# One fused attention, feed-forward and expert kernel: a longer first chunk of the feed-forward, other routing groups, and zero products between the first attention steps

## The chip, the core and the metric

The kernel runs on one core of one Trainium2 chip, in one launch. The metric is the time of that launch on the device in microseconds (us). Five instruction streams run beside each other and wait for each other on semaphores: TensorE (PE in the profile, its weight loads PEld), VectorE (DVE), ScalarE (ACT), GpSimd (POOL) and SyncE (SP, which issues most DMAs). Each stream is executed in its written order.

## The reference

Three stages follow each other; everything is float32. N is 1536 tokens of 512 numbers.

```python
# 1 attention, 2 x 8 heads x 768 x 64: 8 global keys and a local window of 96, linear bias
scores = scale * q @ k.T + bias;  scores = where(keep, scores, -1e9)
a = exp(scores - max);  a = a / (sum(a) + 1e-9);  x = a @ v        # -> 1536 x 512
# 2 gated feed-forward, d_ff = 1536
xn = x / sqrt(mean(x * x) + 1e-6) * rms_g
x = (silu(xn @ w_gate) * (xn @ w_val)) @ w_out
# 3 the two best of 8 experts, 512 -> 1024 -> 512
noisy = x @ w_gate2 + log1p(exp(x @ w_noise)) * noise
top2 = the two largest of noisy;  weight = softmax over the two
out[token] += weight * (relu(x @ w1[e]) @ w2[e])                   # for both experts e
```

## The kernel before

Tokens are handled in 12 tiles of 128 rows. A product of high accuracy is made of three products of two halves each (high x high, high x low, low x high), so most of what TensorE does comes in threes.

**Order of the work.** The program is written with pools of tiles; a scheduler with a timeline of its own estimates (a list scheduler) then decides the order of the instructions on each engine. What the source fixes is what is to be computed, what depends on what, which buffer pool a tile takes, and in which order the pieces get their priority. The order that it made is known before anything runs and can be printed; the times that it had in mind are not used here.

**Attention** is cut into 48 units (tile, pair of heads), which `slot` emits in four steps that lag behind each other: `prep` (L313, transposes of K and Q), `scores` (L363 products `ps`, then VectorE adds the bias and takes the row maximum, L367, then ScalarE's exponential), `turn` (L383, transposes `pp` of the probabilities, copied out by ScalarE and VectorE) and `values` (L428 or L432, products `po`). The first START = 12 units run with nothing else on TensorE ("wide"; they may use more PSUM banks). After that, units are laid between the products of the feed-forward.

**Feed-forward.** d_ff is 12 blocks of 128. The blocks are grouped in CHUNKS; a visit is (chunk, first tile, number of tiles), and VISITS lists them. For each block of a visit `up` makes the gate and value products (L592), `hidden` the gated value on ScalarE and VectorE (`u`, then `dh` and `dl`, its two halves), and `down` the products with w_out (L619), which collect in PSUM over the blocks of the chunk and are then added to the tile's sum `x2` (L629). Chunk 0 takes two tiles per visit (256 columns per product) and runs beside the attention; the later chunks mostly take four tiles (512 columns). The weights come as 64-bit words; `conv` takes them apart on ScalarE, VectorE and GpSimd, and FEED says how many pieces each visit converts. Converted weights lie in pool "a" and, once attention is finished and its memory free, in pool "b" (NRAW says how many).

**Routing.** The tiles are routed in groups GS. `route(g)` follows the last `down` of its tiles: transposes of x2 (L669), router logits `lg` (L673), two ScalarE functions with table loads, the two best of eight on VectorE (`ny` to `chosen`, `sel`), products with a triangle of ones that count how many tokens each expert has before this one (L700 to L703), the slot number `si`, and one indirect DMA per tile and choice from GpSimd that scatters token number and weight to a table in DRAM (L749, `metad`). After group LEAD = 1 (tiles 0 to 7) the kernel counts which expert leads (L715, `lead`), SP loads that number, and unit 0 is prepared: SP fetches the leader's first 256 table entries (`me`, L788, which waits for the scatters), VectorE makes the indices `ic` (L797), GpSimd gathers the rows of x2 (L806), TensorE transposes them (L816).

**Experts.** Unit 0 is the leader's first 256 slots and unit 1 the rest of it; the other experts follow. Unit 1's list must hold tokens of the very last group, which `late_slots` patches in (L644 to L658: `idf` reads the fetched `me`, four comparisons `hot`, 16 small products). Weights of a unit come by SP into raw slots `wab` (L772, L775) and are split into halves (`sa`, `sb`, L576 and L578).

All DMAs of SP stand in one stream: the stores of x2 to DRAM (L632), the fetches of `me` and the weights. A waiting one holds up all that follow.

Of the kernel before, what the change touches and what calls it, by code (L numbers as in the profile page):

```python
# [19 lines left out]
P = 128  # L20
# [85 lines left out]
def fused(ctx: ExitStack, tc: tile.TileContext, q, k, v, n_global, n_local, w_gate, w_val, w_out,  # L106
# [12 lines left out]
    FB2 = F2 // P  # L119
    GS = [4, 4, 2, 2]  # L120
    NG = len(GS)
    G0 = [sum(GS[:g]) for g in range(NG)]
    LEAD = 1
    ST = 4
    CHUNKS = [[0, 1, 2], [3, 4, 5], [6, 7], [8, 9, 10, 11]]
    VISITS = [(0, 2 * i, 2) for i in range(6)] + [(1, 4 * i, 4) for i in range(3)]
    VISITS += [(c, t, 4) for c in (2, 3) for t in (0, 4)] + [(2, 8, 4), (3, 8, 2), (3, 10, 2)]
    FEED = [0, 0, 1, 0, 2, 2, 2, 2, 2, 3, 3]
    START = 12
    LAG = 8  # L130
    NRAW = {"a": 12, "b": 8}
    NACC = 8
# [71 lines left out]
    def small_loads():  # L204
        nc.scalar.dma_start(grow, rms_g.rearrange("(o d) -> o d", o=1).broadcast_to([P, DM]))
        nc.scalar.dma_start(wr[:, :, :E], w_router.rearrange("(c p) e -> p c e", p=P))
        nc.scalar.dma_start(wr[:, :, E:], w_noise.rearrange("(c p) e -> p c e", p=P))
        nc.scalar.dma_start(nz, noise.rearrange("(t p) e -> p t e", p=P))
    tri = sb.tile([P, P], BF16, name="tri")
    ones = sb.tile([P, P], BF16, name="ones")  # L210
# [54 lines left out]
    def bank(kind, wide, name):  # L265
        tags = {"s": ("g", "s"), "t": ("t", "t2", "v"), "o": ("o", "d")} if wide else {"s": ("s",), "t": ("t", "t2"), "o": ("o",)}
        cyc[kind] += 1
        tag = tags[kind][cyc[kind] % len(tags[kind])]
        return ps.tile([P, 512], F32, name=name, tag=tag, bufs=2 if tag == "d" else 1)
# [77 lines left out]
    def scores(u, wide):  # L347
# [9 lines left out]
        for t in range(2):  # L357
            h = pair[pr][t]
            sl = slice((h % 2) * D, (h % 2 + 1) * D)
            o = psc[:, t * W:(t + 1) * W]  # L360
            prods = ((0, 0), (1, 0), (0, 1)) if ti >= F32T else ((0, 0),)
            for n, (a, c) in enumerate(prods):
                nc.tensor.matmul(o, qT[a][sl, h // 2, :], kT[c][sl, h // 2, C0:], start=(n == 0), stop=(n == len(prods) - 1))  # L363
        for t in range(2):
# [10 lines left out]
    def turn(u, wide):  # L375
# [5 lines left out]
        for t in range(2):  # L381
            for j in range(nblk):
                nc.tensor.transpose(p4[:, t, j, :], pp[t][:, j * P:(j + 1) * P], ident)  # L383
        if ti < F32T:
# [143 lines left out]
    def conv(nm, f, src):  # L528
# [11 lines left out]
        sh = nc.vector.tensor_scalar(wi, wi, 3, 0x3FFFFFF8, op0=ALU.logical_shift_left, op1=ALU.bitwise_and)  # L540
        if late:
            after(ab, "A", 1)
            after(sh, "V", 1)
        nc.vector.scalar_tensor_tensor(wi, hi, -0x40000000, wi, op0=ALU.bitwise_and, op1=ALU.bitwise_or)
# [50 lines left out]
    def hidden(ci, f, t0, nt, pg, pv):  # L595
        GN = nt * P
        hp = pools.get("b", at)
        wd = 512 if "b" in pools else 256
        u = hp.tile([P, wd], F32, name=f"u{t0}_{f}", tag="u", bufs=1)[:, :GN]
        nc.scalar.activation(u, pg, AF.Tanh, scale=0.5)  # L600
        nc.vector.scalar_tensor_tensor(u, u, 1.0, pg, op0=ALU.add, op1=ALU.mult)
        nc.vector.scalar_tensor_tensor(u, u, 0.5, pv, op0=ALU.mult, op1=ALU.mult)  # L602
        dh = hp.tile([P, wd], F32R, name=f"dh{t0}_{f}", tag="dh", bufs=2)
        dl = hp.tile([P, wd], F32R, name=f"dl{t0}_{f}", tag="dl", bufs=2)
        nc.scalar.activation(dh[:, :GN], u, AF.Copy)  # L605
        (nc.gpsimd if ci < len(CHUNKS) - 1 else nc.vector).tensor_sub(dl[:, :GN], u, dh[:, :GN].bitcast(F32))  # L606
        return dh, dl

    def down(ci, t0, nt, f, d):
# [12 lines left out]
        for t in range(nt):  # L622
# [7 lines left out]
            if ci == len(CHUNKS) - 1:  # L630
                x2t[ti] = accs[ti]
                nc.sync.dma_start(x2d[ti * P:(ti + 1) * P, :], accs[ti])  # L632
        if t0 + nt == NT // P:
# [26 lines left out]
    def route(g):  # L660
# [3 lines left out]
        for t in range(GT):  # L664
            ti = G0[g] + t
            pt = ps.tile([P, 512], F32, name=f"pr{ti}", tag="ts"[t % 2 if last else 0])
            p3 = pt.rearrange("p (a b) -> p a b", a=DC)
# [241 lines left out]
    while n < START:  # L909
        slot(n, 0)  # L910
        slot(n, 1)
        if n in (3, 6, 9):
            feed(3)
        n += 1
    prev = None
    todo = []
# [13 lines left out]
    def finish(ci, t0, nt, f, d):  # L930
        down(ci, t0, nt, f, d)
        if ci == len(CHUNKS) - 1 and f == CHUNKS[ci][-1] and t0 != G0[-1]:
            g = G0.index(t0)
            route(g)
            if g == LEAD:
                r = nc.sync.value_load(lead.bitcast(I32)[:1, :1], min_val=0, max_val=E - 1)
                units[0].e = units[1].e = r
            if g == LEAD + 1:
                units[1].fetch()

    for vi, (ci, t0, nt) in enumerate(VISITS):
# [9 lines left out]
        for f in CHUNKS[ci]:  # L951
# [19 lines left out]
            prev = (ci, t0, nt, f, d)  # L971
            if (ci, t0) == (2, 8):
                if f == CHUNKS[ci][1]:
                    units[0].slots()
                    units[0].gather(0)
                    units[0].gather(1)
            if ci == 3 and t0 >= 8:
                k = CHUNKS[ci].index(f) + (4 if t0 == 10 else 0)
                if k in (2, 3):
                    units[0].turn(k - 2)  # L980
                moe2_weights(0, units[0].e, k)
    finish(*prev)
# [116 lines left out]
```

## Time and profile before

| what | value |
|---|---|
| median of 3 runs | 856.24 us (855.93 to 857.28) |
| profiled execution | 857.62 us |
| its span, first to last instruction | 855.8 us |
| TensorE busy | 802.3 us (94%) |
| VectorE, ScalarE, GpSimd busy | 54%, 41%, 36% |
| mean granted TensorE clock | 0.960 |

A granted clock of 1.00 in a row is TensorE's full level, 0.50 the lower one; a value between is a mean over both. TensorE's busy time counts an instruction's whole stay in the pipeline, so that a busy engine may still make half its products when the clock is low. The clock of a window is 1.00, too, in the first 36 us, where the trace holds no record of it; there the durations tell it. A row's idle time in square brackets stands just before the instruction, with what ended it.

### The profile page before, as it was taken

The page shows a single profiled execution, that of the slowest core. Times are in us where ns is not written, and L with a number is a line of the kernel's source. Part 1 is how long each engine was busy: PE and PEld are TensorE (multiplying, and loading weights), DVE is VectorE, ACT ScalarE, POOL GpSimd, SP SyncE. Part 2 cuts the span into 40 slices and gives each one's busy share as a digit, 9 for nine tenths or more (in the row PEclk, how much of TensorE's full clock was granted, in tenths as well). Part 3 has the DMA queues.
Part 4 walks back from the last instruction along what each step waited for, and adds up shares of the span by engine and source line. Part 5 has one row for each costly group of instructions (what it writes and reads, how often), then busy time and mean ns, then how long its engine had stood idle before and what let it go on. Part 6 is the DMA issues. An engine that isn't in the chain of part 4 may idle for free. (4 is left out here: it accounts for less than half of the span.)

```text
span 855.8 us, 13326 instructions
## 1 busy us (share of the span) xinstructions
PE 802.3 (94%) x4824; PEld 700.5 (82%) x4824; DVE 462.7 (54%) x1032; ACT 350.6 (41%) x780; POOL 304.7 (36%) x340
## 2 busy tenths in 40 slices
PE   5999999999899999999999777999999999999993
PEld 4678889888778888888889566888899999999982
DVE  3867855675688766323345344654445454545551
ACT  4656665565453332111313252553334343343440
POOL 5335532231665553000053233341242433435321
PEclk9969998999899999999999895999999999999997
DMA  9424431170132420001010505477072829082710
GB/s 200 138 75 136 123 76 26 39 198 2 53 120 99 146 62 15 1 1 50 1 51 21 155 23 124 161 217 221 25 245 77 246 81 278 36 272 91 237 44 33
DMA packets 117125, 89.79 MB, mean 105 GB/s; under 512 B 49481, under 2 KB 100681, under 8 KB 117056
## 3 DMA queue, kind: packets, MB, share of 16 engines
q1 hardware_dynamic: 106864, 68.24, 28.4%
q0 software_dynamic: 7440, 20.32, 7.0%
q10 hardware_dynamic: 2752, 0.34, 0.3%
q8 instruction: 40, 0.66, 0.3%
q14 instruction: 29, 0.24, 0.1%
HBM read 76.23 MB, written 13.34 MB: 105 GB/s over the span
## 5 line engine op out<-in xcount | busy, mean ns | idle before, releaser
L842 PE MATMUL pz<-gh,sa 128*128 128x256 f32 (+7 forms) x576 | 160.1, 344 | 10.1 <-issue 8.6
L842 PEld LDWEIGHTS pz<-gh,sa 128*128 128x128 f32 x576 | 105.6, 192 | 17.0 <-issue 8.6
L842 PE MATMUL pz<-gl,sa 128*128 128x256 f32 (+7 forms) x288 | 98.4, 342 | 0.0
L619 PE MATMUL acc<-wo,dh 128*128 128x512 f32 x288 | 89.3, 403 | 2.8 <-ACT dh L605 2.8
L858 PE MATMUL ac<-zh,sb 128*128 128x480 f32 (+4 forms) x320 | 85.8, 361 | 0.0
L606 POOL TENSOR_TENSOR dl<-u,dh 128x256 fp32r<-128x256 f32 (+1 forms) x33 | 35.4, 1074 | 130.9 <-ACT dh L605 122.2
L846 ACT ACTIVATE zh<-pz 128x256 fp32r<-128x256 f32 (+7 forms) x72 | 35.1, 487 | 108.6 <-PE pz L842 94.8
L847 DVE SCALAR_TENSOR_TENSOR zl<-pz,zh 128x256 fp32r<-128x256 f32 (+7 forms) x72 | 39.7, 552 | 68.4 <-ACT zh L846 55.4
L576 ACT ACTIVATE sa<-wab 128x512 fp32r<-128x512 f32 x72 | 45.3, 629 | 76.2 <-PE ac L858 19.4
L578 POOL TENSOR_TENSOR sa<-wab,sa 128x512 fp32r<-128x512 f32 x21 | 27.1, 1290 | 119.0 <-ACT sa L576 118.1
L619 PEld LDWEIGHTS acc<-wo,dh 128*128 128x128 f32 x288 | 53.0, 191 | 14.1 <-ACT dh L605 3.0
L578 DVE TENSOR_TENSOR sa<-wab,sa 128x512 fp32r<-128x512 f32 x51 | 36.5, 716 | 49.1 <-ACT sa L576 38.5
L592 PE MATMUL pg<-xTh,wg 128*128 128x512 f32 x184 | 62.0, 398 | 0.2 <-DVE u L602 0.2
L592 PE MATMUL pv<-xTh,wv 128*128 128x512 f32 x184 | 61.7, 396 | 0.0
L858 PEld LDWEIGHTS ac<-zh,sb 128*128 128x128 f32 x320 | 59.0, 188 | 3.0
L842 PEld LDWEIGHTS pz<-gl,sa 128*128 128x128 f32 x288 | 55.2, 192 | 2.7
L363 PE MATMUL ps<-kT,qT 64*128 64x256 f32 (+1 forms) x248 | 54.2, 368 | 2.1 <-DVE mx L367 1.4
L619 PE MATMUL acc<-wo,dl 128*128 128x512 f32 x144 | 54.6, 405 | 0.0
L370 ACT ACTIVATE p<-s,mx 128x256 f32<-128x256 f32 (+1 forms) x96 | 46.2, 483 | 19.6 <-DVE mx L367 19.3
L864 PE MATMUL ac<-sb,zh 128*128 128x512 f32 (+1 forms) x160 | 51.4, 407 | 1.4 <-ACT sb L576 1.4
L858 PE MATMUL ac<-zl,sb 128*128 128x480 f32 (+4 forms) x160 | 52.7, 358 | 0.0
L578 DVE TENSOR_TENSOR sb<-wab,sb 128x512 fp32r<-128x512 f32 x67 | 46.7, 697 | 7.6 <-ACT sb L576 7.0
(227 smaller groups left out, 1855.9 us busy)
## 6 DMA issues: line engine op xcount, KB each, us to landing
wab<-in_moe_w_dram SPq DMA_DIRECT2D x128, 256.0 KB
rg<-in_moe_w_gate_dram SPq DMA_DIRECT2D x12, 512.0 KB
rv<-in_moe_w_val_dram SPq DMA_DIRECT2D x12, 512.0 KB
ro<-in_moe_w_out_dram SPq DMA_DIRECT2D x12, 512.0 KB
kn<-in_k_dram SPq DMA_DIRECT2D x12, 256.0 KB
qn<-in_q_dram SPq DMA_DIRECT2D x12, 256.0 KB
vn<-in_v_dram SPq DMA_DIRECT2D x12, 256.0 KB
out_dram<-zero SPq DMA_DIRECT2D x1, 3072.0 KB
```

What stands on the lines that cost most here:

```text
L363: nc.tensor.matmul(o, qT[a][sl, h // 2, :], kT[c][sl, h // 2, C0:], start=(n == 0), stop=(n == len(prods) - 1))
L370: nc.scalar.activation(p[:, :W], s[:, :W], AF.Exp, scale=-1.0, bias=mx[:, h:h + 1], accum_out=sm[:, h:h + 1])
L576: nc.scalar.activation(wp[:, 0], src, AF.Copy)
L578: (nc.gpsimd if pool else nc.vector).tensor_sub(wp[:, 1], src, wp[:, 0].bitcast(F32))
L592: nc.tensor.matmul(pz, a[:, cs], x[:, tt:tt + nt, c, :], start=(n == 0), stop=(n == 3 * DC - 1))
L606: (nc.gpsimd if ci < len(CHUNKS) - 1 else nc.vector).tensor_sub(dl[:, :GN], u, dh[:, :GN].bitcast(F32))
L619: nc.tensor.matmul(acc[t], a[:, tt], w, start=(f == CHUNKS[ci][0] and n == 0), stop=(end and n == 2))
L842: nc.tensor.matmul(pz[:, :cap], a[:, cs], x[:, c, :cap], start=(k == 0), stop=(k == 3 * DC - 1))
L846: nc.scalar.activation(dh[:, :cap], pz[:, :cap], AF.Relu)
L847: nc.vector.scalar_tensor_tensor(dl[:, :cap], pz[:, :cap], 0.0, dh[:, :cap].bitcast(F32), op0=ALU.max, op1=ALU.subtract)
L858: nc.tensor.matmul(acc[c][:, :cap], w[:, c * P:(c + 1) * P], a[:, :cap], start=(f == 0 and k == 0), stop=(f == FB2 - 1 and k == 2))
L864: nc.tensor.matmul(acc[s][:m], a[:, ss], w, start=(f == 0 and k == 0), stop=(f == FB2 - 1 and k == 2))
```

## The change

- Chunks and visits: chunk 0 gets four blocks instead of three, chunk 1 two (blocks 4 and 5). The visits (3, 4) and (2, 8) of four tiles become two visits of two tiles each. FEED and NRAW follow.
- Two-tile visits take their `u`, `dh` and `dl` always from the pool `sb`, no longer from the pool that opens when attention has ended.
- `conv` of block 1 is ordered behind the normalisation of tile 0, that of block 2 behind tile 1, that of later blocks behind tile 2 (before: from block 2 on behind tile 1).
- Routing groups of 4, 2, 2, 2 and 2 tiles instead of 4, 4, 2 and 2; LEAD is 2, which again means tiles 0 to 7.
- On SP, two pairs of unit 0's weights are issued as soon as the leader is known, ahead of the fetch of `me`; the other six follow during visits (2, 10) and (3, 8) instead of (3, 8) and (3, 10).
- The stores of x2 are issued by ScalarE.
- In the first 12 units `busy` puts three products of a zero 128 x 128 by a zero 128 x 512 bf16 tile behind each unit's score products and behind its transposes (12 + 11 times, 69 products). They write PSUM bank "v", which the wide transposes no longer use (two banks instead of three).

```diff
-    GS = [4, 4, 2, 2]
+    GS = [4, 2, 2, 2, 2]
-    LEAD = 1
+    LEAD = 2
-    CHUNKS = [[0, 1, 2], [3, 4, 5], [6, 7], [8, 9, 10, 11]]
+    CHUNKS = [[0, 1, 2, 3], [4, 5], [6, 7], [8, 9, 10, 11]]
-    VISITS += [(c, t, 4) for c in (2, 3) for t in (0, 4)] + [(2, 8, 4), (3, 8, 2), (3, 10, 2)]
-    FEED = [0, 0, 1, 0, 2, 2, 2, 2, 2, 3, 3]
+    VISITS += [(2, 0, 4), (2, 4, 4), (3, 0, 4)] + [(c, t, 2) for c, t in ((3, 4), (3, 6), (2, 8), (2, 10), (3, 8), (3, 10))]
+    FEED = [1, 0, 0, 0, 1, 1, 3, 2, 2, 2, 3]
-    NRAW = {"a": 12, "b": 8}
+    NRAW = {"a": 12, "b": 7}
...
+    blank = sb.tile([P, 512], BF16, name="blank")
+    nc.gpsimd.memset(blank, 0.0)
+    def busy(k, behind):
+        pz = ps.tile([P, 512], F32, name=f"idle{behind.ins.name}", tag="v")
+        for _ in range(k):
+            follow(nc.tensor.matmul(pz, blank[:, :P], blank, start=True, stop=True).ins, behind.ins)
...
-        tags = {"s": ("g", "s"), "t": ("t", "t2", "v"), "o": ("o", "d")} if wide else ...
+        tags = {"s": ("g", "s"), "t": ("t", "t2"), "o": ("o", "d")} if wide else ...
...
+        if wide:
+            busy(3, mm)                     # in scores() and in turn()
...
-        if late:
-            after(ab, "A", 1)
-            after(sh, "V", 1)
+        if f:
+            after(ab, "A", min(f, 3) - 1)
+            after(sh, "V", min(f, 3) - 1)
...
-        hp = pools.get("b", at)
+        hp = pools["b"] if nt > 2 else sb
...
-                nc.sync.dma_start(x2d[ti * P:(ti + 1) * P, :], accs[ti])
+                nc.scalar.dma_start(x2d[ti * P:(ti + 1) * P, :], accs[ti])
...
+    FEEDS = {x: k for k, x in enumerate([(2, 10, 6), (2, 10, 7)] + [(3, 8, f) for f in CHUNKS[3]])}
...
                 units[0].e = units[1].e = r
+                for f2 in range(2):
+                    moe2_weights(0, r, f2)
...
-                moe2_weights(0, units[0].e, k)
+            if kx is not None and kx < FB2 - 2:
+                moe2_weights(0, units[0].e, kx + 2)
```

On SP, around the load of the leader's number, stood before (`x2d` is the store of a tile, `me0` the fetch of the list, `wab0_f` a weight pair of unit 0):

```order
L936 TENSOR_LOAD lead_135
L936 ISA x2
L632 DMA x2d_110<-x2_8_3296 128x512
L632 DMA x2d_110<-x2_9_3298 128x512
L788 ISA
L788 DMA me0_4956<-metad_111 128x2x2
L772 ISA
L772 DMA wab0_0_5015<-in_moe2_w1_dram 128x4x128
```

and stands now:

```order
L949 TENSOR_LOAD lead_137
L949 ISA x2
L784 ISA
L784 DMA wab0_0_5252<-in_moe2_w1_dram 128x4x128
L787 ISA
L787 DMA wab0_0_5252<-in_moe2_w2_dram 128x512
L784 ISA
L784 DMA wab0_1_5255<-in_moe2_w1_dram 128x4x128
L787 ISA
L787 DMA wab0_1_5255<-in_moe2_w2_dram 128x512
L800 ISA
L800 DMA me0_5340<-metad_111 128x2x2
```

Two weight pairs stand where two stores stood; the fetch of `me0` comes behind them, and the second list's fetch `me1`, which stood before the last four pairs, now stands behind all eight.

On TensorE, the count of the leader stood among the up products of the last visit (3, 10), in its first block 8 (`pz10_8`):

```order
L592 MATMUL pz10_8_5160<-xTl2_2272,wv8_3583 128x256
L592 MATMUL pz10_8_5160<-xTh2_2271,wv8_3583 128x256 x2
L715 LDWEIGHTS ones_115
L715 MATMUL lg1_4757<-selsum_146,ones_115 128x8
L592 MATMUL pz10_8_5160<-xTl2_2272,wv8_3583 128x256
```

and stands now one visit earlier, at the second block 9 of visit (3, 8) (`pz8_9`), among the last down products of (2, 10):

```order
L605 MATMUL pz8_9_5441<-xTl2_2466,wg9_3987 128x256
L631 MATMUL acc2_10_5386<-wo7_3843,dh10_7_5382 128x512 x2
L727 LDWEIGHTS ones_117
L727 MATMUL lg2_5152<-selsum_148,ones_117 128x8
L631 MATMUL acc2_11_5387<-wo7_3843,dh10_7_5382 128x512 x2
```

So three blocks more of the feed-forward stand behind the count.

On VectorE, in the last routing group, `idf`, which reads the fetched `me1`, stood behind the logits, at the slot number:

```order
L729 TENSOR_TENSOR oe3_5475<-chosen_131,pe3_5470 128x2x8 x2
L644 CAST idf_5492<-me1_5281 128x2
L731 TENSOR_REDUCE sl3_5478<-oe3_5475 128x4
L733 CAST si3_5480<-sl3_5478 128x4
L578 TENSOR_TENSOR sa0_4_0_5718<-wab0_4_5283,sa0_4_0_5718 128x512
```

and stands now ahead of that group's logits `ny4`:

```order
L641 TENSOR_TENSOR x2_11_3739<-x2_11_3739,acc3_11_5740 128x512
L591 TENSOR_TENSOR sa0_3_0_6100<-wab0_3_5394,sa0_3_0_6100 128x512
L859 SCALAR_TENSOR_TENSOR zl0_2_6088<-pz0_2_6074,zh0_2_6087 128x256
L656 CAST idf_5903<-me1_5704 128x2
L695 TENSOR_TENSOR ny4_5858<-ny4_5858,nz_113 128x16
L696 TENSOR_TENSOR ny4_5858<-ny4_5858,lg4_5835 128x16
```

The wait for `me1` has moved from behind the choice of the experts to ahead of it.

## Rows read from the trace of the kernel before

**Rows 1.** Windows: length, busy us (count) of PE, PEld, DVE, ACT, POOL, clock, DMA.
```profile
22.00:36.00 14.00, 13.83 (x51) 10.36 (x52) 11.58 (x33) 9.03 (x28) 5.75 (x6) 1.00 0.63 171
36.00:49.60 13.60, 11.03 (x78) 8.83 (x77) 13.31 (x34) 10.20 (x29) 7.02 (x7) 1.00 0.51 152
49.60:66.60 17.00, 17.00 (x66) 14.05 (x66) 9.56 (x26) 7.41 (x22) 3.52 (x5) 0.50 0.15 41
...
126.00:135.00 9.00, 8.69 (x50) 7.69 (x51) 4.22 (x17) 4.13 (x15) 4.88 (x8) 0.62 0.22 46
...
205.00:224.00 19.00, 13.76 (x156) 12.16 (x154) 12.18 (x32) 10.57 (x28) 6.53 (x8) 0.82 0.01 2
224.00:464.00 240.00, 239.78 (x1200) 198.53 (x1200) 132.83 (x240) 72.73 (x128) 79.83 (x72) 1.00 0.16 53
464.00:483.00 19.00, 15.10 (x101) 13.33 (x101) 6.83 (x21) 2.97 (x8) 7.99 (x9) 1.00 0.36 77
483.00:510.40 27.40, 22.09 (x143) 18.57 (x141) 14.18 (x57) 14.89 (x28) 9.72 (x10) 0.88 0.30 102
510.40:531.00 20.60, 12.04 (x49) 11.08 (x48) 6.59 (x25) 3.76 (x8) 8.42 (x8) 0.50 0.52 120
```

**Rows 2.** Transposes L383 in 24:35.5 and 36:49.6, first product L592: ns min/median/max.
```profile
L383 PE MATMUL pp<-ident,p x8: 418/421/474, 28.7 to 34.9; 128*128 128x128 f32 x8
...
L383 PE MATMUL pp<-ident,p x16: 272/273/329, 35.9 to 46.3; 128*128 128x128 f32 x16
...
L592 PE MATMUL pz<-xTh,wg x2: 415/488/562, 64.5 to 65.9; 128*128 128x256 f32 x2
```

**Rows 3.** TensorE at 512 and 256 columns (windows at full clock), and 512 columns later.
```profile
340.00:360.00 20.00, 20.00 (x88) 1.00 0.00 1
457.16:459.40 2.24, 2.24 (x20) 1.00 0.00 0
...
528.61 0.63 PE L864 MATMUL ac<-sb,zh 128*128 128x512 f32 x1
529.03 0.63 PE L864 MATMUL ac<-sb,zl 128*128 128x512 f32 x1
```

**Rows 4.** Timeline of TensorE's first product after the attention.
```profile
219.11 0.58 PE L592 MATMUL pz<-xTh,wg 128*128 128x256 f32 x1 [2.69 <-DVE u L602]
```

**Rows 5.** Timelines of GpSimd, SP, VectorE and ScalarE around the lists.
```profile
461.92 0.99 POOL L749 DMA_INDIRECT metad<-meta,si  x1 [19.02 <-DVE si L733]
...
505.43 1.01 POOL L749 DMA_INDIRECT metad<-meta,si  x1 [1.57 <-DVE si L733]
...
477.93 0.41 SPq L788 DMA_DIRECT2D me<-metad  x1
...
514.56 0.39 SPq L788 DMA_DIRECT2D me<-metad  x1
...
479.77 0.17 DVE L797 TENSOR_SCALAR ic<-me 128x2 int32<-128x2 int32 x1 [3.99 <-DMA me<-metad]
...
497.93 0.17 DVE L683 TENSOR_TENSOR ny<-ny,nz 128x16 f32<-128x16 f32 x1 [1.28 <-ACT ny L682]
...
516.49 0.17 DVE L644 CAST idf<-me 128x2 f32<-128x2 int32 x1 [5.14 <-DMA me<-metad]
...
481.42 0.63 ACT L576 ACTIVATE sa<-wab 128x512 fp32r<-128x512 f32 x1 [5.15 <-DMA wab<-in_moe_w_dram]
```

**Rows 6.** Timeline of TensorE in the routing: start, length, instruction, [idle before <- what ended it].
```profile
459.41 0.18 PE L700 MATMUL lg<-sel,tri 128*128 128x8 bf16 x1
...
482.40 1.54 PE L619 MATMUL acc<-wo,dh 128*128 128x512 f32 x4 [2.75 <-ACT dh L605]
486.40 1.09 PE L816 MATMUL pg<-ident,xg 128*128 128x128 f32 x4 [1.61 <-DMA xg<-x2d,ic]
...
489.82 0.74 PE L619 MATMUL acc<-wo,dl 128*128 128x512 f32 x2
...
518.96 0.58 PE L842 MATMUL pz<-gh,sa 128*128 128x256 f32 x1 [8.55 <-issue]
```

More of the change, by code (lines that the diff above doesn't have):

```diff
@@ L265, in bank @@
     def bank(kind, wide, name):
-        tags = {"s": ("g", "s"), "t": ("t", "t2", "v"), "o": ("o", "d")} if wide else {"s": ("s",), "t": ("t", "t2"), "o": ("o",)}
+        tags = {"s": ("g", "s"), "t": ("t", "t2"), "o": ("o", "d")} if wide else {"s": ("s",), "t": ("t", "t2"), "o": ("o",)}
         cyc[kind] += 1
@@ L362, in scores @@
             for n, (a, c) in enumerate(prods):
[L363 removed]
+                mm = nc.tensor.matmul(o, qT[a][sl, h // 2, :], kT[c][sl, h // 2, C0:], start=(n == 0), stop=(n == len(prods) - 1))
+        if wide:
+            busy(3, mm)
         for t in range(2):
@@ L382, in turn @@
             for j in range(nblk):
-                nc.tensor.transpose(p4[:, t, j, :], pp[t][:, j * P:(j + 1) * P], ident)
+                mm = nc.tensor.transpose(p4[:, t, j, :], pp[t][:, j * P:(j + 1) * P], ident)
+        if wide:
+            busy(3, mm)
         if ti < F32T:
@@ L596, in hidden @@
         GN = nt * P
-        hp = pools.get("b", at)
-        wd = 512 if "b" in pools else 256
-        u = hp.tile([P, wd], F32, name=f"u{t0}_{f}", tag="u", bufs=1)[:, :GN]
+        hp = pools["b"] if nt > 2 else sb
+        u = hp.tile([P, GN], F32, name=f"u{t0}_{f}", tag="u", bufs=1)
         nc.scalar.activation(u, pg, AF.Tanh, scale=0.5)
@@ L602, in hidden @@
         nc.vector.scalar_tensor_tensor(u, u, 0.5, pv, op0=ALU.mult, op1=ALU.mult)
[L603 to L606, printed above, removed]
+        dh = hp.tile([P, GN], F32R, name=f"dh{t0}_{f}", tag="dh", bufs=2)
+        dl = hp.tile([P, GN], F32R, name=f"dl{t0}_{f}", tag="dl", bufs=2)
+        nc.scalar.activation(dh, u, AF.Copy)
+        (nc.gpsimd if ci < len(CHUNKS) - 1 else nc.vector).tensor_sub(dl, u, dh.bitcast(F32))
         return dh, dl
@@ L665, in route @@
             ti = G0[g] + t
-            pt = ps.tile([P, 512], F32, name=f"pr{ti}", tag="ts"[t % 2 if last else 0])
+            pt = ps.tile([P, 512], F32, name=f"pr{ti}", tag=("t", "t2", "s")[t % 3])
             p3 = pt.rearrange("p (a b) -> p a b", a=DC)
@@ L971, in fused @@
             prev = (ci, t0, nt, f, d)
[L972 to L980, printed above, removed]
-                moe2_weights(0, units[0].e, k)
+            kx = FEEDS.get((ci, t0, f))
+            if kx == 0:
+                units[0].slots()
+                units[0].gather(0)
+                units[0].gather(1)
+            if kx in (3, 4):
+                units[0].turn(kx - 3)
+            if kx is not None and kx < FB2 - 2:
+                moe2_weights(0, units[0].e, kx + 2)
     finish(*prev)
```

## The prediction, made before the changed kernel ran

> **What bounds the kernel now.** I read the shares of busy time first, then the windows by stage, then the waits inside the stages that are not full. TensorE is busy 94% of the span, so what can be won is time in which it stands still or runs at the lower clock. [Rows 1] show where that is. From 224 to 464 it is busy 239.78 of 240 us at the full clock: nothing to win, and an instruction added there costs its whole length. Elsewhere two things are lost: the idle time (window less busy), and of a busy stretch at clock 0.50 one half.
>
> - Start. Before 36 us the trace has no clock record, but the transposes L383 take 421 ns against 273 ns behind 35.9 [rows 2], so the clock is low up to there. Then it is full until 49.6, and low again until 66.6, where TensorE is busy 17.00 of 17.00 us: it is the bound, and only for its clock. From 36 to 49.6 VectorE is busy 13.31 of 13.60: the bound there is VectorE, and TensorE is idle 2.57 us.
> - 126 to 135: idle 0.31 us, and 0.38 of clock missing over 9 us is 3.4 us; 3.7 lost.
> - 205 to 224, the end of attention: idle 5.24 us, of which 2.69 is one product that waits for room for the next `u` [rows 4], and some 2.3 us at the low clock (0.18 of 19 us, less its idle part); 7.5 lost.
> - Routing, 464 to 531: idle 3.90 + 5.31 + 8.56 = 17.77 us. The low clock costs half of 510 to 531 (12.04 busy, 6.0 lost) and 0.12 of 483 to 510, less the idle time in it (2.6). Together 26.4.
>
> The routing is a chain through all engines [rows 5, 6]: counting products (459.41), first scatter (461.92), 16.0 us until SP issues the fetch of `me` behind eight scatters, 1.84 to `ic`, 6.63 over the gather to the transposes at 486.40. Beside it ScalarE stands 5.15 us for its first weights, which SP issues behind that fetch, and so TensorE stands 2.75 us at 482.40 for a `dh` that ScalarE has not made. Later VectorE stands 5.14 us at `idf` for the second list, and the last four weight pairs, behind that list on SP, leave TensorE 8.55 us without work.
>
> **The change, part by part.**
>
> *Longer first chunk.* The first chunk's groups of four blocks reach over the end of attention, and two-tile visits take `u` from a pool that is always open, so the wait of rows 4 goes. I take 6 of the 7.5 us (0 if attention's last chain is late in any case, 7.5 if all goes). The middle loss of 3.7 comes from a wait of an attention step; with one third more feed-forward work per visit between the steps I take 2 (0 to 3.7). Against it, two visits of four tiles become pairs: 432 products of 256 columns for 216 of 512. One takes 2.24/20 = 0.112 us, one of 512 columns 20.00/88 = 0.227 [rows 3]: by that nothing is lost. That window holds few changes of bank or weights; a little more, 0.116 to 0.117, is my estimate for longer stretches, so +1.0 (0 to +1.9).
>
> *Routing groups, count and weights.* The count now stands three blocks earlier: 96 products of 0.117 and 27 of 0.23, that is 17.4 us of work, lie between it and the first transposes, and 2.9 between the group's counting products and the count; TensorE is there 20.3 us after them. The list: 2.5 to the first scatter, then four scatters instead of eight. The second list of before had four, and took 516.49 - 505.43 = 11.06 us to its reader; the first took 17.85 with eight. I take 12.5, as weights are now ahead of the fetch, and 6.6 to the transposes: 21.6. TensorE waits 1.3 us (0; or 6.4 if the list takes 17.6). ScalarE's wait for `wab` goes, since two pairs are on their way before the list; what is late next is that list.
>
> In the last group `idf` stands ahead of `ny4`. The second list lands 2.5 + 11.06 us after the counting products of tiles 8 and 9, which stand 3.5 us of work ahead of the last down product, so 10.1 us after that one. VectorE reached `ny` 7.4 us after it (489.82 + 0.74 to 497.93), so it will stand at `idf`, and behind it are queued the choice of the experts, the counting products and the patch of unit 1. TensorE has 10.6 us of products until it asks for the choice: I count 1.3 us (0 to 5.14, the wait of before). The last scatters, 11 us of chain and the gather then come 2.5 us late for unit 1's rows (0 to 8.55, the wait they take the place of; the weights no longer stand behind this list). With 2 us of small waits and one stretch at the low clock (3.4) the stage loses 10.5 instead of 26.4: -16 (-7 to -24).
>
> The Trainium skill, "DMA: Bandwidth & Descriptors", section "Queues, rings and completion order", speaks against the new place of the weights: engines serve their queues' packets in turn, so four weight transfers ahead of the fetch share the engines with the scatters. Rows 5 bound that without it: between the fetch at 477.93 and the first weights in use at 481.42 lie 3.5 us, and so much the list could be late.
>
> *ScalarE's stores.* ScalarE is busy 72.73 of 240 us before the routing [rows 1], nothing waits for these twelve issues but the gather: 0 (up to +1).
>
> *Zero products.* 69 of them, 128 x 512. At the full clock 0.23 us each, 15.9 in all; at the low clock 0.42, the step between the two rows at 528.61, 29.5 in all [rows 3]. They are worth something only where they keep the clock full. From 22 to 36 TensorE is busy 13.83 of 14 us and VectorE 11.58: with the full clock the stretch falls to VectorE's time, -2. From 36 to 49.6 VectorE bounds: 0, the products (about 3.7 us) fill idle time. From 49.6 to 66.6, 17.0 us of work at half speed are 8.5 at full, and some 20 products add 4.6: 13.1, -3.9; VectorE's 9.56 lies below. The first eight groups run at the low clock before it rises: +1.8 beyond the idle time; one more weight piece is converted early: +1. Start: -3. Bounds: -10.1, if all VectorE idle time of these windows goes (2.42 + 0.29 + 7.44), and +26.8, if all run low on a full engine (29.5 less 2.7 idle). I stay near the windows' own work, since both ends need one state throughout. The last two groups stand behind the first up product, at 0.23 each: +1.4.
>
> **Sum.** -3 - 2 - 6 - 16 + 1 + 1.4 = -24.6 (rounded parts; taken as -24.5) against the profiled execution's 857.62: 833.1. The median of the runs shown is 1.4 below that execution, so 832.
>
> **Rivals.**
>
> *The lists still set the end of the routing.* For it: every term there is a chain of DMAs with waits that order alone doesn't shorten, and `idf` stands ahead of more. Against it: four scatters fewer, and 17.4 us of cover. If 4.4 us stay at the first list (2.75 + 1.61), 8.55 at the second and the 6.0 of its clock, 7.5 are saved instead of 16: 840.
>
> *The start gains nothing.* At 49.6 the full clock was lost behind a stretch in which TensorE had 2.57 us of idle time; the wide transposes now have two banks instead of three, and so may wait more. Then -3 becomes +2: 837. The Trainium skill, "TensorE: Matmul & The Clock Gate", section "A second HAM failure mode: psum-queue depth-cycling", says that going round PSUM banks with short idle spells lets the clock swing between its levels; the trace agrees in so far as the clock fell at 49.6 while TensorE was busy 11.03 of 13.60. Its price is this rival's.
>
> *The weights ahead of the list make it late*, by 3.5 us and a low stretch of 3.4: 838.
>
> *All holes vanish*: routing -24, tail -7.5, middle -3.7, start -5 and the same costs: 818.
>
> *Slower: the zero products run at the low clock and TensorE stays the bound.* The place is 10 to 66 us, where it is full already at that clock. +26.8, and the stretch from 36 to 49.6 loses the full clock too, about +5; the other parts give -21.6: 857.62 + 10.2 - 1.4 = 866. It decides from the point where these products cost more than the 21.6 won elsewhere: some 45 of the 69 at 0.42 on a full engine with the full stretch lost. For it: TensorE was fully busy from 49.6 to 66.6 and the clock stayed low for all of it. Against it: the clock rose at 35.9 with less work.
>
> **How the numbers follow.** Forecast 832: 0.55, with 822 to 842 as its own range. Lists 0.17 (840), start 0.12 (837), late list 0.03 (838), all holes 0.03 (818), slower side 0.10 (866; a tenth to a fifth of it ends near no change). The range 820 to 848 leaves out the slow case, the best one and a little of the lists' worst. About 0.2% is what a measurement of this kernel can tell from no change: faster 0.89, same 0.03, slower 0.08.
>
> **What would show it.** Right: full clock from some 20 us on, and the first up product clearly before 64.5 [rows 2]; no wait of 2.69 at the end of attention; TensorE's waits at the first list's transposes and at the last choice near 1 to 2 us; no 8.55 gap; the fetch of `me` some 5 us earlier behind its first scatter. Wrong: a second stretch at clock 0.50 before 66 us, a VectorE that stands at `idf` for 5 us or more with TensorE idle behind it, ScalarE late with `dh` while weights still travel, or more than 20 us lost between the last attention step and unit 1.

## The result, and the profile after

| what | before | after |
|---|---|---|
| median of four runs | 856.76 us (855.93 to 857.67) | 828.67 us (827.88 to 829.82) |
| ratio, 95% interval | | 0.9711 (0.9655 to 0.9766) |
| profiled execution, its span | 857.62, 855.8 us | 829.82, 828.1 us |
| mean granted TensorE clock | 0.960 | 0.985 |

The kernel became 28 us faster; 832 was forecast. Run again later beside other kernels, the changed kernel took 832.8 us (829.66 to 837.23, ratio 0.976, 0.9709 to 0.9812). Its mean granted clock differed from execution to execution (0.977 to 0.985), and the interval of its ratio is 4.4 us to either side, so kernels that did not run beside each other are told apart by time only from some 5 us on; below that I go by the traces, and each is of one execution.

The busy shares barely moved; the clock line of the 40 slices did. This is the page of the changed kernel:

```profile
PE 789.2 (95%) x5105; PEld 698.3 (84%) x5105; DVE 459.0 (55%) x1071; ACT 356.6 (43%) x803; POOL 304.6 (37%) x346
PE   6999999999989999999999988999999999999993
PEclk9999999999999999999999998999999999999997
```

Windows of the changed kernel in the form of [rows 1]; up to 66.6 us the windows are the same, behind that they follow its own stages (attention now ends at 225, the routing begins at 380):

```profile
10.00:22.00 12.00, 10.81 (x57) 6.67 (x58) 7.50 (x28) 6.55 (x23) 5.74 (x11) 1.00 1.23 251
22.00:36.00 14.00, 13.94 (x93) 9.80 (x91) 12.02 (x37) 10.90 (x32) 4.83 (x6) 1.00 0.60 166
36.00:49.60 13.60, 13.08 (x80) 8.73 (x77) 10.56 (x31) 8.81 (x26) 7.68 (x10) 1.00 0.55 152
49.60:66.60 17.00, 17.00 (x129) 14.55 (x128) 12.05 (x33) 11.16 (x32) 6.65 (x8) 1.00 0.50 130
...
126.00:135.00 9.00, 9.00 (x87) 8.01 (x85) 5.02 (x18) 5.40 (x19) 5.72 (x8) 1.00 0.06 13
205.00:224.00 19.00, 19.00 (x197) 17.31 (x196) 10.56 (x31) 8.68 (x25) 2.02 (x3) 1.00 0.01 2
224.00:254.00 30.00, 25.77 (x179) 22.04 (x178) 17.71 (x29) 13.12 (x27) 17.89 (x19) 0.94 0.25 72
254.00:380.00 126.00, 126.00 (x577) 103.05 (x575) 84.12 (x113) 41.64 (x72) 50.55 (x45) 1.00 0.23 75
380.00:430.00 50.00, 48.96 (x370) 46.21 (x371) 17.85 (x87) 17.12 (x35) 13.48 (x14) 0.97 0.10 22
430.00:465.00 35.00, 32.14 (x233) 29.05 (x231) 19.76 (x64) 10.10 (x23) 10.65 (x11) 1.00 0.56 163
465.00:517.00 52.00, 45.60 (x305) 41.50 (x303) 27.12 (x105) 23.11 (x46) 17.13 (x16) 0.93 0.14 25
517.00:816.00 299.00, 296.26 (x1610) 274.02 (x1608) 145.89 (x239) 119.67 (x225) 110.80 (x103) 1.00 0.52 160
```

From 49.6 to 66.6 us TensorE is busy for all 17.00 us in both kernels, but runs 129 instructions where it ran 66: that is the clock. Its transposes and zero products show when it rose. The first row is of the time up to 14.3 us, the second from there to 49.6; the others are zero products in the timeline (start, length), three, one and three:

```profile
L394 PE MATMUL pp<-ident,p x2: 417/445/473, 13.7 to 13.9; 128*128 128x128 f32 x2
L394 PE MATMUL pp<-ident,p x31: 272/273/417, 13.9 to 45.5; 128*128 128x128 f32 x31
...
11.11 1.46 PE L216 MATMUL idleI-190_191<-blank 128*128 128x512 bf16 x3
18.50 0.38 PE L216 MATMUL idleI-251_252<-blank 128*128 128x512 bf16 x1
18.93 0.81 PE L216 MATMUL idleI-262_263<-blank 128*128 128x512 bf16 x3
```

Three products take 0.81 us, one alone 0.38, so the step is (0.81 - 0.38) / 2 = 0.215 us, and 69 are 14.9 us. The first up product comes at 57.0 us (64.5 before, [rows 2]).

The sum over the windows, idle time and half of the busy time at the low clock together:

| stretch | lost before | lost after | change |
|---|---|---|---|
| 10 to 66.6 us | 25.2 | 3.9 | -21.3, +14.9 for the products: -6.4 |
| rest of attention and its end (before to 224, after to 254) | 12.0 | 5.9 | -6.1 |
| feed-forward and routing (before to 531, after to 517) | 26.5 | 15.0 | -11.5 |
| experts to the last product (it ends at 841.4 before, at 813.7 after) | 2.2 | 0.4 | -1.8 |
| behind the last product | 14.4 | 14.4 | 0 |

Together -25.8 of the 27.7 us by which the span fell. The other 1.9 us lie in no window's idle time or clock. The row of the routing is that of this execution: in the second trace of the same kernel (the changed kernel again, below, with a span of 832.8) the stage, there from 254 to 521, loses 20.1 instead of 15.0.

The routing after, in the form of [rows 5, 6]: first GpSimd, SP, ScalarE and VectorE, then TensorE's longest waits.

```profile
437.51 0.99 POOL L761 DMA_INDIRECT metad<-meta,si  x1 [0.30 <-DVE si L745]
441.37 0.97 POOL L761 DMA_INDIRECT metad<-meta,si  x1 [0.30 <-issue]
...
448.90 0.37 SPq L800 DMA_DIRECT2D me<-metad  x1
...
447.43 0.63 ACT L589 ACTIVATE sa<-wab 128x512 fp32r<-128x512 f32 x1 [3.77 <-DMA wab<-in_moe_w_dram]
...
450.70 0.93 DVE L809 TENSOR_SCALAR ic<-me 128x2 int32<-128x2 int32 x1 [0.25 <-DMA me<-metad]
490.16 0.17 DVE L656 CAST idf<-me 128x2 f32<-128x2 int32 x1 [5.22 <-DMA me<-metad]
490.24 0.17 DVE L695 TENSOR_TENSOR ny<-ny,nz 128x16 f32<-128x16 f32 x1
```

```profile
448.42 1.20 PE L631 MATMUL acc<-wo,dh 128*128 128x512 f32 x4 [1.83 <-ACT dh L617]
461.19 0.63 PE L828 MATMUL pg<-ident,xg 128*128 128x128 f32 x4 [0.71 <-DMA xg<-x2d,ic]
492.53 0.51 PE L854 MATMUL pz<-gh,sa 128*128 128x256 f32 x2 [2.29 <-DVE sa L591]
510.07 1.94 PE L828 MATMUL pg<-ident,xg 128*128 128x128 f32 x8 [4.11 <-DMA xg<-x2d,ic]
```

The 8.55 us for the last weights are gone; what is late now is ScalarE's first weights (3.77, TensorE 1.83 behind them) and the rows of unit 1 (4.11).

### The profile page after: what moved, and what is told of

Read it like the earlier page. It is cut to its first block, busy times and chain, and to the rows that moved or that the text cites. A ratio compares the mean times of both kernels' runs of the same rounds, so it can differ in the third digit from the quotient of the medians.

```text
span 828.1 us, 13951 instructions
## 1 busy us (share of the span) xinstructions
PE 789.2 (95%) x5105; PEld 698.3 (84%) x5105; DVE 459.0 (55%) x1071; ACT 356.6 (43%) x803; POOL 304.6 (37%) x346
## 5 line engine op out<-in xcount | busy, mean ns | idle before, releaser
L854 PE MATMUL pz<-gh,sa 128*128 128x256 f32 (+7 forms) x576 | 158.3, 340 | 2.3 <-DVE sa L591 2.3
L605 PE MATMUL pz<-xTh,wv 128*128 128x256 f32 x352 | 74.7, 288 | 0.0
L605 PE MATMUL pz<-xTh,wg 128*128 128x256 f32 x352 | 72.8, 285 | 1.4 <-DVE u L614 0.7
L605 PEld LDWEIGHTS pz<-xTh,wg 128*128 128x128 f32 x352 | 58.3, 190 | 5.1 <-DVE u L614 1.3
L631 PEld LDWEIGHTS acc<-wo,dh 128*128 128x128 f32 x288 | 51.0, 188 | 13.0 <-ACT dh L617 3.3
L605 PEld LDWEIGHTS pz<-xTh,wv 128*128 128x128 f32 x352 | 58.4, 191 | 0.8 <-issue 0.3
L761 POOL DMA_INDIRECT metad<-meta,si x24 | 24.4, 1019 | 94.2 <-DVE si L745 87.4
```

Of the source, the lines that this page charges most:

```text
L605: nc.tensor.matmul(pz, a[:, cs], x[:, tt:tt + nt, c, :], start=(n == 0), stop=(n == 3 * DC - 1))
L631: nc.tensor.matmul(acc[t], a[:, tt], w, start=(f == CHUNKS[ci][0] and n == 0), stop=(end and n == 2))
L761: st = nc.gpsimd.indirect_dma_start(out=metad, out_offset=bass.IndirectOffsetOnAxis(ap=si[:, t, kk:kk + 1], axis=0), in_=meta[:, G0[g] + t ...
L854: nc.tensor.matmul(pz[:, :cap], a[:, cs], x[:, c, :cap], start=(k == 0), stop=(k == 3 * DC - 1))
```

## The experiments

Ratios are to the kernel before, run beside each of them; the changed kernel stands at 0.971 and, run again, 0.976.

**No zero products.** `busy(3, mm)` becomes `busy(0, mm)`.

```diff
-            busy(3, mm)
+            busy(0, mm)
```

> The changed kernel without its 69 zero products (the order of the first attention steps is made anew without them). My theory: they cost 69 x 0.2155 = 14.9 us of TensorE and give back 21.3 us of TensorE's losses between 10 and 66.6 us (25.2 before, 3.9 after), so without them the kernel takes about 6 us more than the changed one: 835 us, with the low clock back in the first 60 us. Rival: the clock rises for another reason (the order of the attention steps, the longer first chunk) and the products only cost their time: 814 us. Second rival: without them the clock stays low for longer than it did before: 845 us or more.

Measured: 844.58 us, 0.9879 (0.9835 to 0.9923). By the ratios it is 10 to 14 us slower than the changed kernel, some twice what I expected. Its windows (same columns) and two of TensorE's waits:

```profile
22.00:36.00 14.00, 11.29 (x38) 7.82 (x39) 9.19 (x25) 7.84 (x23) 4.70 (x6) 1.00 0.52 151
36.00:49.60 13.60, 13.50 (x78) 11.52 (x76) 11.35 (x31) 9.05 (x24) 4.76 (x5) 1.00 0.38 111
...
240.64 0.74 PE L518 MATMUL px<-ident,x 128*128 128x128 f32 x4 [3.58 <-DVE x L505]
256.42 0.38 PE L607 MATMUL pz<-xTh,wg 128*128 128x256 f32 x1 [1.65 <-DVE u L616]
```

The clock rose at 43.0 us instead of 14.3. The span is 14.6 us longer (842.7 against 828.1). Up to 66.6 us this kernel loses 16.0 us more than the changed one (19.9 against 3.9) and saves 14.9: there the products only just pay. The rest came later. Some 5 us are waits and a stretch at the low clock at the end of attention (3.58 and 1.65 against single waits up to 0.69 there, besides 2.24 at 249.5), 2 us lie among the experts, and the other 6.6 are in no idle time and no low clock: TensorE counts as fully busy at the full clock from 66.6 to 224 us in both kernels, yet ends the last transposes of attention 10 us later (241.4 against 231.4), and the wait of 3.58 just ahead of them is not half of that. The scheduler makes the order anew without the products; that this order costs the 13.5 us is my reading, and what made the 6.6 stays open. The first rival (they only cost) is out.

**One product in each place.**

```diff
-            busy(3, mm)
+            busy(1, mm)
```

> The changed kernel with one zero product in each place instead of three (23 instead of 69; the order of the first attention steps is made anew). They cost 5.0 us instead of 14.9. My theory: the clock needs an unbroken stream on TensorE only to rise; with a third of the products it rises later and is lost again somewhere before 66 us, which gives back about half of what is saved: 824 us. Rival: the number doesn't matter once the clock is up: 819 us. Second rival: the clock stays low as without them: 840 us.

Measured: 845.64 us, 0.9909 (0.9868 to 0.995): as slow as with none. The windows show why:

```profile
22.00:36.00 14.00, 9.74 (x46) 6.63 (x46) 9.01 (x24) 7.71 (x23) 4.51 (x6) 0.96 0.51 146
36.00:49.60 13.60, 12.71 (x68) 9.90 (x68) 11.40 (x31) 8.35 (x23) 3.85 (x4) 0.79 0.39 104
```

TensorE is busy 9.74 of 14 us from 22 to 36 (13.94 with three products), and the full clock, first recorded at 28.0 us, was lost again from 34.8 to 41.7. That the clock would rise later and be lost again was right; my price, "half of it back", was wrong. Up to 66.6 us this kernel loses 16.6 us, against 19.9 with no products and 3.9 with three, and pays 5.0 for 23 products. The second rival came near in the time, but its clock, as low as with none, is not what the trace shows. Here, too, the later order differs, so the 846 us are not the clock's alone.

**The zero products alone, in the kernel before** (with two banks for the wide transposes).

```diff
+    blank = sb.tile([P, 512], BF16, name="blank")
...
+        if wide:
+            busy(3, mm)
-        tags = {..., "t": ("t", "t2", "v"), ...
+        tags = {..., "t": ("t", "t2"), ...
```

> The kernel before, with the zero products and the two banks for wide transposes as the only change. My theory: the same exchange of 21.3 us for 14.9, so 6 us faster than before: 850 us, with the clock full from some 15 us on. Rival: the first chunk of three blocks has too little work to use the full clock, VectorE bounds the first 66 us, and the products cost as much as they give: 856 us. Second rival: the clock falls again once the products end, behind 60 us: 860 us.

Measured: 851.73 us, 0.9973 (0.9949 to 0.9997); span 849.9 against 855.8.

```profile
36.00:49.60 13.60, 12.60 (x79) 8.85 (x80) 10.71 (x31) 8.87 (x24) 7.46 (x9) 1.00 0.56 155
49.60:66.60 17.00, 17.00 (x124) 14.05 (x123) 12.91 (x35) 11.33 (x33) 6.35 (x8) 1.00 0.43 118
```

The clock was full from 16.4 to 207.6 us; the start loses 5.2 us instead of 25.2. Twenty won, 14.9 paid: 5 us, as the span shows; the timing says 0 to 4. This is the plain price of this part, and it is small.

**The first chunk of three blocks again, all else as changed.**

```diff
-    CHUNKS = [[0, 1, 2, 3], [4, 5], [6, 7], [8, 9, 10, 11]]
+    CHUNKS = [[0, 1, 2], [3, 4, 5], [6, 7], [8, 9, 10, 11]]
-    FEED = [1, 0, 0, 0, 1, 1, 3, 2, 2, 2, 3]
+    FEED = [0, 0, 1, 0, 2, 2, 2, 2, 2, 3, 3]
```

> The changed kernel with chunks of 3, 3, 2 and 4 blocks and their old feed of weight pieces; the pool for two-tile visits, the zero products, routing groups and weights stay. My theory: at the end of attention the groups of a fourth block gave TensorE work, so a loss of some 9 us comes back there (11.0 us from 66 to 224 us in the kernel before with zero products) in place of the 5.9 that the changed kernel loses from 224 to 260: 4 us slower than the changed kernel, 833 us. Rival: the always open pool alone removed the wait, and the fourth block gave nothing: 829 us. Second rival: the fourth block costs, because chunk 0's products have 256 columns: 826 us.

Measured: 851.59 us, 0.9986 (0.9948 to 1.0025). Nearly the whole gain is gone, five times what I gave this part.

```profile
66.60:126.00 59.40, 57.60 (x413) 49.85 (x412) 38.52 (x109) 31.68 (x93) 22.23 (x30) 0.89 0.29 75
126.00:224.00 98.00, 95.39 (x999) 83.45 (x997) 62.52 (x184) 57.56 (x165) 28.37 (x43) 1.00 0.28 69
224.00:270.00 46.00, 39.03 (x187) 32.51 (x188) 27.88 (x42) 19.56 (x38) 25.69 (x26) 0.89 0.31 92
...
228.02 1.09 PE L516 MATMUL px<-ident,x 128*128 128x128 f32 x4 [4.99 <-DVE x L503]
```

The always open pool did remove the 2.69 us wait of [rows 4], so that rival's mechanism works, but a wait of 4.99 for the last normalised tile stands there now, and the low clock comes back at 92 and 225 us. A hole costs twice, by itself and by the clock behind it: from 66.6 to 126 us TensorE is idle for 1.80 us and at the low clock for 13.7. From 66.6 to 254 this kernel loses 21.6 us and the changed one 5.9, which is 15.7 of the 23.8 us between their spans. That is not the price of the fourth block alone, though: the kernel before with zero products has three blocks, too, kept the full clock to 207.6 and lost 11.0 there. Half of the 21.6 thus comes from three blocks together with the rest of the change (the pool, the order of `conv`, the visits), and no run here separates these.

**The routing groups as before.**

```diff
-    GS = [4, 2, 2, 2, 2]
+    GS = [4, 4, 2, 2]
-    LEAD = 2
+    LEAD = 1
-    ... (3, 0, 4)] + [(c, t, 2) for c, t in ((3, 4), (3, 6), (2, 8), (2, 10), (3, 8), (3, 10))]
+    ... [(c, t, 4) for c in (2, 3) for t in (0, 4)] + [(2, 8, 4), (3, 8, 2), (3, 10, 2)]
```

> The changed kernel with the routing groups 4, 4, 2 and 2, the leader after the second, and visits (3, 4) and (2, 8) of four tiles again; zero products, first chunk of four and weights ahead of the fetch stay. My theory: eight scatters lie ahead of the first list again (5 us) with less work to cover them, and the last group's list is late, so the routing loses 22 to 26 us of TensorE instead of 15: 836 us. Rival: the weights ahead of the fetch are what helped, the groups gave nothing: 829 us.

Measured: 842.79 us, 0.9857 (0.9806 to 0.9908), by the ratios 8 to 13 us slower. TensorE's waits of over 1 us in the routing:

```profile
455.43 1.20 PE L631 MATMUL acc<-wo,dh 128*128 128x512 f32 x4 [2.60 <-ACT dh L617]
471.42 0.63 PE L828 MATMUL pg<-ident,xg 128*128 128x128 f32 x4 [2.05 <-DMA xg<-x2d,ic]
498.02 0.80 PE L876 MATMUL ac<-sb,zh 128*128 128x512 f32 x1 [1.83 <-POOL sb L591]
517.08 1.97 PE L828 MATMUL pg<-ident,xg 128*128 128x128 f32 x8 [5.56 <-DMA xg<-x2d,ic]
534.68 0.63 PE L828 MATMUL pg<-ident,xg 128*128 128x128 f32 x4 [3.15 <-DMA xg<-x2d,ic]
```

Counted as above, it loses 28.1 us from 420 to 540 (the changed kernel 12.6), and up to 250 us the two run alike (first product of 512 columns at 249.9 and 249.5). My theory holds on the place and the direction. What the routing gained belongs to the groups with the visits that go with them, not to the two weight pairs ahead of the fetch, which this kernel has, too; groups and visits are not told apart.

**Weights behind the list's fetch.** Only some rows around the fetch move.

```diff
-                for f2 in range(2):
-                    moe2_weights(0, r, f2)
...
+            if kx == 0:
+                moe2_weights(0, units[0].e, 0)
+                moe2_weights(0, units[0].e, 1)
```

> The changed kernel, with unit 0's first two weight pairs issued behind the fetch of the list instead of ahead of it; nearly all other rows of the order stay. My theory: the fetch waits for the scatters in either case (it was issued 4.7 us after the last of the four weight transfers), so the list comes no earlier by more than 0.5 us, while the weights come some 6 us later, ScalarE stands in front of them and TensorE behind its half: 5 to 6 us more than the changed kernel, 834 us, 838 with a stretch at the low clock. Rival (the weights ahead slow the scatters and the list): the list comes 2 to 3.5 us earlier, which pays for the later weights: 829 us or less.

Measured: 831.22 us, 0.9732 (0.9674 to 0.9789), the same as the changed kernel; span 828.6 against 828.1.

```profile
436.12 0.99 POOL L761 DMA_INDIRECT metad<-meta,si  x1 [0.30 <-DVE si L745]
...
445.16 0.40 SPq L800 DMA_DIRECT2D me<-metad  x1
...
447.26 0.17 DVE L809 TENSOR_SCALAR ic<-me 128x2 int32<-128x2 int32 x1 [4.17 <-DMA me<-metad]
...
448.70 0.63 ACT L589 ACTIVATE sa<-wab 128x512 fp32r<-128x512 f32 x1 [5.15 <-DMA wab<-in_moe_w_dram]
```

From the first scatter to the list's reader it is 11.1 us here and 13.2 in the changed kernel: with the weights ahead, the fetch waited 7.5 us from the last scatter's start (5.2 here), though SP had issued the last of the four transfers 4.7 us before. Three later traces with the weights ahead bear this out: in the changed kernel run again, `idf` late and the gathers first the fetch waited 8.7, 8.2 and 8.8 us. And the weights, counted from the first scatter, come only 2.7 us later when issued behind (12.6 against 9.9). Both of my numbers failed, and the rival is right on the list (2.1 us). By time the two kernels are not told apart. The Trainium skill, "DMA: Bandwidth & Descriptors", section "Queues, rings and completion order", says that each DMA engine takes turns between the packets of the queues it has work for; the trace agrees as far as the fetch, which waits for the scatters, went 2.3 us later beside the weights.

**The stores on SP.**

```diff
-                nc.scalar.dma_start(x2d[ti * P:(ti + 1) * P, :], accs[ti])
+                nc.sync.dma_start(x2d[ti * P:(ti + 1) * P, :], accs[ti])
```

> The changed kernel with the stores of x2 issued by SP again; the rest of the order stays but for some rows. My theory: nothing waits for ScalarE's issues, so nothing changes: within 1 us of the changed kernel, 829 us. Rival: on SP two stores wait for tiles 8 to 11 in front of the weights and the second list, which then come later: 831 to 833 us.

Measured: 836.45 us, 0.9803 (0.9723 to 0.9882), but its profiled execution took 825.46, with a span of 823.7 and the clock at 0.989. TensorE's waits in that trace are near those of the changed kernel (2.42 behind `dh`, 2.29 behind `sa`). SP itself stands up to 20.4 us at a store, as the rival has it, but its last store is out by 478.0 us, and the second list's fetch behind it goes at 484.7, after 6.5 us of waiting for the scatters. So no list is late there for a store. By time it is inconclusive: the changed kernel run again spread over much of the same range.

**Ten products more, ahead of everything.**

```diff
+    pz0 = ps.tile([P, 512], F32, name="warmup", tag="v")
+    for _ in range(10):
+        nc.tensor.matmul(pz0, blank[:, :P], blank, start=True, stop=True)
```

> The changed kernel with ten more zero products that stand first on TensorE, in the time from 2 to 6.5 us in which it waits for the first K tile. My theory: the clock rises some 4 to 5 us earlier than at 14.3 us, which gives back up to half of that as TensorE's time: 2 us faster, 827 us. Rival: VectorE and the first transfers set the pace until 20 us and TensorE only waits longer: 829 us. Second rival: the waits between the first transposes let the clock rise no earlier, and the products in front delay the first transposes: 830 us.

Measured: 836.20 us, 0.9813 (0.9726 to 0.9899). The clock rose at 5.4 us, as hoped, but in the order made anew TensorE stood before the second K tile, and the clock fell again from 19.0 to 25.9:

```profile
20.24 0.48 PE L325 MATMUL pt<-ident,kn 128*128 128x128 f32 x1 [5.76 <-DMA kn<-in_k_dram]
```

No gain is seen; the theory failed on the transfers.

**The changed kernel again, `idf` late, and the gathers first.** The first has no edit; in the other two VectorE's `idf` follows the choice (first pair of lines), and in the last the scatters of the last group follow unit 1's gathers.

```diff
-        nc.vector.tensor_copy(idf, u.me[:, :ns, 0])
+        follow(nc.vector.tensor_copy(idf, u.me[:, :ns, 0]).ins, slr)
...
+            units[1].slots()
+            gs1 = [units[1].gather(x) for x in range(2)]
...
+                if last:
+                    follow(st.ins, gs1[1].ins)
```

> The changed kernel once more, unaltered, as a measure for its neighbours. My theory: 829 us again, so that the 836 us of the kernel with the stores on SP and of the one with ten products more came from these edits. Rival: its executions, too, spread from 826 to 837 us with the clock that each is granted, and then those two can't be told from it.

> The changed kernel with one row moved: on VectorE, idf stands behind the choice of the experts of the last group again, not ahead of it. In the changed kernel ny4 was ready at 489.1 us and began at 490.2, behind idf. My theory: 1.1 us earlier choice, 1 us faster, 828 us. Rival (my prediction's step: the wait of VectorE at idf, 5.2 us, holds the choice up): 3 to 5 us faster, 825 us.

> The same move of idf, and unit 1's two gathers ahead of the last group's four scatters on GpSimd instead of behind them; nothing else moves. In the changed kernel unit 1's indices were ready at 501.1 us, the gather went at 502.7 behind the scatters, TensorE waited 4.1 us for its rows and the clock was low for 6.8 us. My theory: the rows come 2.7 us earlier in all, the wait falls to some 1.5 us and the low stretch with it: 825 us, 823 if the clock holds. Rival: the scatters, now 4 us later, make unit 2's list late and TensorE waits there instead: 829 us.

Measured beside each other: 832.8 us (0.976, 0.9709 to 0.9812), 831.4 (0.9746, 0.9699 to 0.9793) and 828.2 (0.9706, 0.9658 to 0.9754). TensorE at unit 1's rows in the three:

```profile
514.58 1.73 PE L828 MATMUL pg<-ident,xg 128*128 128x128 f32 x7 [4.40 <-DMA xg<-x2d,ic]
```

```profile
510.71 1.52 PE L828 MATMUL pg<-ident,xg 128*128 128x128 f32 x6 [5.55 <-DMA xg<-x2d,ic]
```

```profile
506.47 0.63 PE L833 MATMUL pg<-ident,xg 128*128 128x128 f32 x4 [0.59 <-DMA xg<-x2d,ic]
...
527.59 0.63 PE L833 MATMUL pg<-ident,xg 128*128 128x128 f32 x4 [2.43 <-DMA xg<-x2d,ic]
```

With `idf` late the wait of TensorE at the choice fell from 3.39 to 0.85 us, and the next wait grew by 1.15, so nearly half was given back. The 2.54 are more than the 1.1 I expected, because in this trace of the changed kernel `idf` held the choice up for longer: `ny` was ready at 490.7 and began at 493.3, 2.6 us later. The gathers took the wait at unit 1 away, and the low clock behind it; of that, 2.43 us came back at the next unit's rows, with a low stretch from 529.0 to 532.4, which is part of the rival. By time the intervals overlap. The spans of the three traces are 832.8, 829.3 and 826.9, but the first trace of the changed kernel has 828.1 and the one with the stores on SP 823.7, so no version is shown to be the faster one.

**The weights' splits behind the feed-forward**, on top of the last.

```diff
+        if u == 0 and f < 2:
+            follow(first.ins, state["hold"])        # dh of the last block of visit (3, 8)
```

> The kernel of gather_first, in which ScalarE (and VectorE and GpSimd behind it) splits unit 0's first weights only behind dh of the last block of visit (3, 8), so that no dh stands behind a wait for weights. In gather_first TensorE waited 3.1 us there, and the clock was low for 6.8 us from 447 on; the first unit's products come 25 us later, so the splits have time. My theory: the leader's list is as late as the weights, so TensorE, 3 us earlier at the list's transposes (which came 0.0 to 0.7 us late in the changed kernel), waits there for some 3 us instead: 0 to 3 us faster than gather_first by the clock alone, 826 us. Rival: the list has 3 us in hand, and wait and low stretch both go: 822 us.

Measured: 831.65 us, 0.9672 (0.9629 to 0.9714; the kernel before took 860.36 beside it).

```profile
452.93 0.39 PE L608 MATMUL pz<-xTh,wg 128*128 128x256 f32 x1 [2.12 <-DVE u L617]
...
451.93 0.17 DVE L818 TENSOR_SCALAR ic<-me 128x2 int32<-128x2 int32 x1 [6.17 <-DMA me<-metad]
```

The 3.1 us behind the weights became 2.1 behind `ic`: VectorE stands in order before the list, and a `u` behind it. The list was as late as the weights, as the theory has it, though the place of the new wait is VectorE, not the transposes; a gain in time is not shown.

## Why the prediction was right, and where its steps were not

The direction and the size came from the right place: TensorE's idle time and its clock, stage by stage. That the time came so near, 828.67 against 832, is in good part luck: the start gave 4.8 us more than its terms, routing and middle 6.4 less, and the experts and the 1.9 us that no window holds were not in the sum. Signs that I had named for being wrong did appear: VectorE stood 5.22 us at `idf` with TensorE idle for 2.29 behind it, and ScalarE was late with a `dh` while weights travelled (1.83). Two slips of the sums change nothing: 69 times 0.42 is 29.0, not 29.5, and the late list's price of 6.9 on 832 gives 839.

- *Start, -3, and +1.4 for late products.* Measured -6.4 together. The full clock came at 14.3 us, so fewer products ran at the low clock than the eight groups I charged (one group of three), and the loss fell by 21.3 us. How much of this is the products' is less plain: in the kernel before they win 20.0 us for 14.9, in the changed one 16.0, and 5.3 of the 21.3 are there without them. The rival that the start gains nothing is out by these windows, and the slower one too: two of the 69 steps, not 45, were at 0.42 (the first group's, (1.46 - 0.63) / 2). The Trainium skill, "TensorE: Matmul & The Clock Gate", section "A second HAM failure mode: psum-queue depth-cycling", ties a swinging clock to going round PSUM banks with short idle spells. This trace does not test that, since the spells are missing: with two banks TensorE was idle for 0.06 and 0.52 us in the windows from 22 to 49.6, and the clock stayed full from 14.3 to 249.8 us.
- *Middle -2 and end of attention -6.* Measured -6.1 of the -8. The waits up to 224 us are gone, as said; 4.2 us of waits and one stretch at the low clock moved behind the end (224 to 254), where weight pieces and the last tile are converted. I had sized this part by its holes in the kernel before. The run with three blocks shows that taking the fourth block out of the changed kernel costs far more, 15.7 us in this stretch; but as the kernel before with zero products lost only 11.0 there with three blocks, the two parts of the change hang together, and the fourth block has no price of its own.
- *Routing -16.* Measured -11.5, and some -6 in the second trace of the same kernel. The term was mis-sized by three of its waits. "ScalarE's wait for `wab` goes" failed: it waited 3.77 us, and TensorE 1.83. The first weights, issued at 441.74 beside the scatters, were used 5.7 us later; issued behind them, in the run above, 2.9 us later (445.80 to 448.70), so I put the wait down to the scatters. The first list's wait was right (0.04 and 0.71 against 1.3), and so was its length (13.2 us against 12.5). The last list came 10.2 us after the start of the last down product (479.95 to 490.16; 10.1 was worked out), yet `ny` was ready on ScalarE at 489.1, so `idf` held it up by 1.1 us and not by the 5.2 that its own row shows (by 2.6 of 5.6 in the second trace); TensorE's wait for the choice was 2.29, where I had counted 1.3. Unit 1's rows came 4.1 us late where I had 2.5, with a stretch at the low clock.
- *ScalarE's stores, 0.* Not contradicted, and not proven.
- *256 columns, +1.* Not settled. This window of the changed kernel holds 64 of them alone:

```profile
232.89:239.97 7.08, 7.08 (x64) 7.08 (x63) 5.07 (x8) 3.69 (x7) 3.84 (x4) 1.00 0.47 148
```

They take 0.111 us each, no more than half of a 512-column product [rows 3]. In the routing, from 449.91 to 452.68, 23 of them stand alone at the full clock, too, and take 0.120 each.

## What to carry to other kernels

Where an engine looks fully busy, count its instructions per microsecond: 66 and 129 in the same 17 us are two different kernels. Filler by itself paid little here, 0 to 4 us in the kernel before: it wins only where it carries the clock to work that can use it. Where a scheduler makes the order anew behind every edit, a run without one part also measures another order, so compare where the time was lost and not only how much. A wait's own length doesn't tell what it costs: `idf` stood 5.2 us and held the choice up by 1.1 (5.6 and 2.6 in another execution), since what stood behind it wasn't ready; find out when that was. Holes filled one by one mostly move (weights, then list, then gather), so follow the chain to the end before giving a gain to one link.

## What the hardware showed that I had not expected

One zero product in each place gave little, three nearly all: up to 66.6 us the loss was 19.9 us with none, 16.6 with one and 3.9 with three; with one, TensorE's busy time from 22 to 36 us was 9.74 of 14 and the full clock was lost again. Four weight transfers issued ahead of a 2 KB fetch made it leave 2.3 us later or more, although its own wait was for the scatters. And executions of one and the same program spread over 829.7 to 837.2 us with a granted clock between 0.985 and 0.977. Two traces of it show where: from 440 to 540 us one loses 12.4 us and the other 19.2. The waits behind `dh` and `sa` were 1.83 and 2.29 us in the first and 3.13 and 3.39 in the second, and only in the second did the clock fall there (447.9 to 454.7 and 495.7 to 499.1).
